# The second product's parts behind every second Strassen product instead of behind each

## The chip, the cores and the metric

One core of a Trainium2 chip runs the whole program. The metric is device time in microseconds (us) from launch to the last output, the median of several runs; three runs of the kernel before gave 844.39 to 845.39 us, median 845.2 us.

## What is computed

```python
ret = (q @ k.T / sqrt(64)) * Dmat          # decayed, causal, per head; B 4, H 8, S 576, D 64
x = (ret @ v), heads side by side          # 2304 tokens x 512
h = x @ w_in;  g = relu(h) ** 2            # 512 -> 2048
x = g @ w_out                              # 2048 -> 512
h = x @ w_in2; g = h * clip(h + 3, 0, 6) / 6
out = g @ w_out2
```

The weights come as 64-bit floats and are decoded on the chip. Every fp32 matrix product of the two layers is made from three matmuls with the operands split into a high and a low part (high x high, high x low, low x high: `PASSES`).

## The kernel before

After the retention the 2304 tokens are worked off in blocks of 768. The first block of layer 1 is done plainly, chunk by chunk. The other five (`BLOCKS`, L21: two of layer 1, three of layer 2) compute the hidden values by Strassen-Winograd's seven products instead of eight. The loop at L1022 runs over 40 pairs k of 128-wide hidden chunks, eight pairs to a block. Pairs 0 to 15 are of layer 1, 16 to 39 of layer 2.

One call of `pair` (L675) issues the seven products P1, P6, P2, P7, P5, P4, P3 in this order, each six matmuls of 384 columns (L690). They go in turn into two PSUM banks, `ta` and `tb` (P1, P2, P5, P3 in the one, P6, P7, P4 in the other), and each is read out right behind its matmuls, in the program's order: ACT copies P1 (`p1`, L725) and P2 (`c11`, L733); DVE adds P6, P7, P5, P4 and P3 to the running sums (L714). From the five sums come the four hidden tiles c11, u3, c21 and c12. `act` (L696) applies the nonlinearity: on ACT alone in layer 1 (L701, L702), on ACT and DVE in layer 2 (L706, L707). ACT then rounds the high part (L708), and DVE makes the low part (L710), one product later (`late`, `flush`): so the low part of c21 is issued on DVE right behind the addition for P3 (c12, L754, L755).

The second matrix product (g @ w_out) of a pair is held in `pending` as **parts** and issued during the next pair, in the gaps between its products, by `between(i)` behind product i. In layer 1 a pair has eight parts of six matmuls (three of 512 columns, three of 256; L478); in layer 2 twelve parts of three matmuls (512 columns; L650). The first half of the parts uses the tile g[1], made from u3 and c21; the second half uses g[0], from c11 and c12. The first matmul of a part reads a high part; the second one, in its operands, a low part. In the last pair of a block the sums of the second product end: these parts are issued in the next pair (k = 8, 16, 24, 32; for the plain block in pair 0), and each is followed by the copy of its PSUM bank to memory, on DVE (L485, L663) or ACT (L486, L490, L667).

`between(i)` also issues `side[i]`: pieces of the preparation of later blocks and of layer 2's weights (decoding, L171 to L190; splitting, L196 and L197; operand sums, L585, L602, L607), and DMAs on SP's queue. Every engine works off its instructions in the written order (`manual_schedule`, L777). Where a part stands therefore decides what PE does between two products, and, in pairs with PSUM copies, also what stands ahead of the next addition on DVE and ACT.

Of the kernel before, what the change touches and what calls it, by code (L numbers as in the profile page):

```python
# [74 lines left out]
def retention_moe_moe2(ctx, tc, qk, qk_last, kv, w_in, w_out, w_in2, w_out2, consts, out):  # L75
# [339 lines left out]
    def load_out(l, key, c):  # L415
        w = wout_place()
        nc.sync.dma_start(out=w.rearrange("p e n -> p (e n)").bitcast(F32), in_=kept["o", l, c])
        wouts[key] = w
# [48 lines left out]
    def y_first(t0, state):  # L467

        def work(w, gt, first, last):
            def step(m):  # L470
                if first and m == 0:
                    state["y"] = [bank(b, [128, 512], "yps") for b in range(KD)]
                    state["y"] += [bank(KD + b, [128, 2, 256], "ytail") for b in range(2)]
                y = state["y"]
                for k, (o, n) in enumerate(PARTS):
                    p = y[KD + m // 2][:, m % 2] if k else y[m]
                    for e, (wp, gpart) in enumerate(PASSES):
                        nc.tensor.matmul(  # L478
                            out=p, lhsT=w[:, wp, m * 128:m * 128 + 128], rhs=gt[:, gpart, o:o + n],
                            start=first and e == 0 and not (k and m % 2), stop=last and e == 2, skip_group_check=k == 1,  # L480
                        )
                if last:
                    dst = xall[:, m, t0:t0 + 512]
                    if m % 2:
                        nc.vector.tensor_copy(dst, y[m])  # L485
                        nc.scalar.activation(  # L486
                            out=xall[:, m - 1:m + 1, t0 + 512:t0 + BLOCK], in_=y[KD + m // 2], func=ACTF.Copy
                        )
                    else:
                        nc.scalar.activation(out=dst, in_=y[m], func=ACTF.Copy)  # L490

            return [lambda m=m: step(m) for m in range(KD)]

        return work
# [118 lines left out]
    def load_left(k):  # L613

        j, p = divmod(k, NPAIR)
        l = BLOCKS[j][0]
        lefts[j, p] = []
        for e in range(4):
            if l == 0 and e > 1:
                t = place(f"w{4 * (k % 2) + e}", [128, 2, 2, 256], F32R, "win")  # L620
                nc.sync.dma_start(
                    out=t[:, 1].rearrange("p a n -> p (a n)").bitcast(F32),
                    in_=kept["f", 0, p][:, 512 * (e - 2):512 * (e - 1)],
                )
                lefts[j, p].append(t.rearrange("p b a n -> p a b n"))
                continue
            only = slice(1, 2) if e == 1 else slice(0, 2)
            t = place(f"w{4 * (k % 2) + e}", [128, 1 if e == 1 else 2, 2, 256], F32R, "win")
            nc.sync.dma_start(
                out=t.bitcast(F32),  # L630
                in_=kept["s", l, p, e].rearrange("p (a b n) -> p a b n", a=2, b=2)[:, only],
            )
            lefts[j, p].append(t)

    def parts_of_left(k, e):

        hi, lo = (lefts[divmod(k, NPAIR)][e][:, :, wp] for wp in range(2))
        return split_parts(hi, lo, lo.bitcast(F32), nc.vector)

    def y_second(j, state):  # L640

        t0, n = BLOCKS[j][1], BLOCK

        def work(w, gt, first, last):
            def step(m):
                if first and m == 0:
                    state["y"] = [bank(b, [128, DM], "yps") for b in range(n // 128)]
                p = state["y"][m]
                for e, (wp, gpart) in enumerate(PASSES):
                    nc.tensor.matmul(  # L650
                        out=p, lhsT=gt[:, gpart, m * 128:m * 128 + 128], rhs=w[:, wp],
                        start=first and e == 0, stop=last and e == 2,
                    )
                if last:
                    if j == len(BLOCKS) - 1 and m < 4:
                        o = place(f"w{m}", [128, DM], F32, "o")
                    else:
                        o = stagep.tile([128, DM], F32, tag="stage", name="o")
                    final = j == len(BLOCKS) - 1
                    for f in range(2 if final and m == n // 128 - 1 else 1):  # L660
                        own = slice(256 * f, 256 * f + 256) if final and m == n // 128 - 1 else slice(0, DM)
                        if (m + f) % 2 == 0:
                            nc.vector.tensor_scalar(  # L663
                                out=o[:, own], in0=p[:, own], scalar1=1.0 / 6.0, scalar2=None, op0=ALU.mult
                            )
                        else:
                            nc.scalar.activation(out=o[:, own], in_=p[:, own], func=ACTF.Copy, scale=1.0 / 6.0)  # L667
                        queue = nc.scalar if final and (m + f) % 2 else nc.sync
                        queue.dma_start(out=out[t0 + m * 128:t0 + m * 128 + 128, own], in_=o[:, own])

            return [lambda m=m: step(m) for m in range(n // 128)]

        return work

    def pair(j, p, flip, between):  # L675

        wl = lefts.pop((j, p))
# [46 lines left out]
        product("P1", ta, True, False)  # L724
        nc.scalar.activation(out=p1, in_=ta, func=ACTF.Copy)  # L725
        between(0)
        tb = bank(b1, [128, HALF], "hps")
        product("P6", tb, True, True)
# [48 lines left out]
    with tc.manual_schedule():  # L777
# [52 lines left out]
        for k in range(2):  # L830
            kind, u, k = order.pop(0)
# [190 lines left out]
        for k in range(total):  # L1022
            j, p = divmod(k, NPAIR)
            l = BLOCKS[j][0]
            if p == 0:
                ywork = y_second(j, {}) if l else y_first(BLOCKS[j][1], {})
            side = [[] for _ in range(7)]


            if j + 1 < len(BLOCKS):  # L1030
                if p == 2:
                    sums, highs2, lows2 = operand_steps(j + 1)
                if 2 <= p < 5:
                    for i, f in zip((1, 4), sums[2 * (p - 2):][:2]):
                        side[i].append(f)
                if p == NPAIR - 1:
                    highs, lows = highs2, lows2
                    for i, at in enumerate((0, 1, 3, 4, 6)):
                        if at < 6:
                            side[at + 1].append(lows[i])  # L1040
                        side[at].append(highs[i])
                    side[6] += sums[6:]
            if p == 0:
                if j:
                    side[0].append(lows[4])
                else:
                    side[0] += sums[6:]
                for i, at in ((5, 1), (6, 3)):
                    side[at].append(highs[i])
                    side[at + 1].append(lows[i])  # L1050
            for i, e in ((4, 1), (6, 0)):
                side[i].append(lambda e=e: load_out(l, (j, 2 * p + e), 2 * p + e))
            if k >= 1 and k + 1 < total:
                side[0].append(lambda: load_left(k + 1))
            if k + 1 < total and BLOCKS[(k + 1) // NPAIR][0] == 0:
                for i, e in ((4, 2), (5, 3)):
                    for n in range(2):
                        side[i + n].append(lambda e=e, n=n: parts_of_left(k + 1, e)[n]())
            if p < NPAIR - 1:
                for i in range(4 if j and not p else 0, 7):  # L1060
                    if slots:
                        side[i] += [store_late] + slots.pop(0)
            elif late_stores:
                side[1].append(store_late)
            count = len(pending)

            def between(i):
                want = count - count * (i + 1) // 7
                while len(pending) > want:
                    pending.pop(0)()  # L1070
                for f in side[i]:
                    f()

            gt = pair(j, p, flip, between)
            flip = not flip
            assert not pending
            for e in (1, 0):
                pending += ywork(
                    wouts[j, 2 * p + e], gt[e], p == 0 and e == 1, p == NPAIR - 1 and e == 0
                )  # L1080
# [37 lines left out]
```

## Time and profile before

| what | value |
|---|---|
| median of 3 runs | 845.2 us (844.39 to 845.39) |
| the profiled execution | 845.26 us, its span 843.5 us |
| PE busy | 825.0 us, 98% of the span |
| DVE, ACT, POOL busy | 586.1 us, 466.6 us, 144.5 us |
| granted TensorE clock | 0.999 |
| pairs 0 to 39 | from 194.7 us on |

The profile has one execution. Times are counted from the first instruction. "Busy" of PE is the union of modelled matmul durations, which overlap: a 384-column matmul is shown with 338 ns, but the next one starts some 175 ns later. So the pace of PE is read from starts, not from durations. A release written behind an arrow ("<-DVE g L710") names the instruction whose end let the waiting one begin.

### The profile page before, as it was taken

The page shows a single profiled execution, that of the slowest core. Times are in us where ns is not written, and L with a number is a line of the kernel's source. Part 1 is how long each engine was busy: PE and PEld are TensorE (multiplying, and loading weights), DVE is VectorE, ACT ScalarE, POOL GpSimd, SP SyncE. Part 2 cuts the span into 40 slices and gives each one's busy share as a digit, 9 for nine tenths or more (in the row PEclk, how much of TensorE's full clock was granted, in tenths as well). Part 3 has the DMA queues.
Part 4 walks back from the last instruction along what each step waited for, and adds up shares of the span by engine and source line. Part 5 has one row for each costly group of instructions (what it writes and reads, how often), then busy time and mean ns, then how long its engine had stood idle before and what let it go on. Part 6 is the DMA issues. An engine that isn't in the chain of part 4 may idle for free.

```text
span 843.5 us, 14173 instructions
## 1 busy us (share of the span) xinstructions
PE 825.0 (98%) x5220; PEld 741.9 (88%) x5220; DVE 586.1 (69%) x1018; ACT 466.6 (55%) x913; POOL 144.5 (17%) x122
## 2 busy tenths in 40 slices
PE   8989999997999999999999999999999999999998
PEld 7878888886999899999999888898898888889886
DVE  5779999999787876887875895546644546534434
ACT  1248777768865876867775653335433345433332
POOL 2353333331332320132230130000000000000000
PEclk9999999999999999999999999999999999999999
DMA  9996788876787894689786688553854552854522
GB/s 364 343 300 221 239 289 282 294 249 242 258 326 275 304 330 177 232 280 362 276 293 266 225 287 312 202 185 137 316 221 163 188 199 87 329 209 161 201 99 75
DMA packets 77963, 206.58 MB, mean 245 GB/s; under 512 B 8005, under 2 KB 24773, under 8 KB 77895
## 3 DMA queue, kind: packets, MB, share of 16 engines
q1 hardware_dynamic: 77314, 204.90, 68.9%
q8 instruction: 41, 0.67, 0.3%
q10 hardware_dynamic: 580, 0.79, 0.3%
q14 instruction: 28, 0.22, 0.1%
HBM read 159.00 MB, written 46.66 MB: 244 GB/s over the span
## 4 chain that ended last, share of the span: by engine, by line
PE 80%; DVE 7%; DMA 6%; ACT 4%; issue 1%; SPq 1%; POOL 0%; DVEq 0%; ACTq 0%; POOLq 0%
PE hps L690 33%; PE yps L650 22%; PE yps L478 13%; PE ytail L478 7%; PE hps L431 5%; DMA kvt<-in_kv_dram 3%; DMA qkt<-in_qk_dram 3%; DVE a L184 1%; DVE g L454 1%; DMA stage<-in_w_out_dram 1%; DVE w L190 1%; DVE a L178 1%; ACT u L706 0%; ACT r L172 0%; DVE u L714 0%
## 5 line engine op out<-in xcount | busy, mean ns | idle before, releaser
L650 PE MATMUL yps<-wo,g 128*128 128x512 f32 x864 | 226.8, 394 | 1.5 <-DVE g L710 1.3
L690 PE MATMUL hps<-xlast,win 128*128 128x384 f32 x960 | 194.9, 338 | 1.7 <-DVE u L714 1.6
L650 PEld LDWEIGHTS yps<-wo,g 128*128 128x128 f32 x864 | 159.4, 188 | 26.0 <-DVE g L710 2.0
L690 PEld LDWEIGHTS hps<-xlast,win 128*128 128x128 f32 x960 | 167.7, 188 | 10.5 <-DVE u L714 2.1
L714 DVE TENSOR_TENSOR u<-hps,u 128x384 f32<-128x384 f32 x120 | 66.8, 557 | 157.1 <-PE hps L690 150.5
L478 PE MATMUL yps<-g,wo 128*128 128x512 f32 x576 | 166.1, 396 | 0.4 <-POOL wo L197 0.4
L690 PE MATMUL hps<-xop,win 128*128 128x384 f32 x720 | 146.4, 338 | 3.7 <-ACT r L447 3.4
L690 PEld LDWEIGHTS hps<-xop,win 128*128 128x128 f32 x720 | 125.7, 188 | 10.7 <-ACT r L447 3.6
L708 ACT ACTIVATE g<-c 128x384 fp32r<-128x384 f32 x120 | 63.1, 525 | 88.1 <-DVE c L707 86.6
L478 PEld LDWEIGHTS yps<-g,wo 128*128 128x128 f32 x576 | 101.8, 188 | 10.2 <-POOL wo L197 0.8
L478 PEld LDWEIGHTS ytail<-g,wo 128*128 128x128 f32 x576 | 94.0, 188 | 17.3
L478 PE MATMUL ytail<-g,wo 128*128 128x256 f32 x576 | 98.5, 279 | 0.0
L710 DVE TENSOR_TENSOR g<-c,g 128x384 fp32r<-128x384 f32 x120 | 67.9, 566 | 11.3 <-ACT g L708 11.1
L431 PE MATMUL hps<-xring,win 128*128 128x512 f32 (+1 forms) x384 | 69.7, 338 | 0.3 <-ACT r L447 0.2
L733 ACT ACTIVATE c<-hps 128x384 f32<-128x384 f32 x40 | 19.7, 492 | 90.9 <-PE hps L690 90.9
L431 PEld LDWEIGHTS hps<-xring,win 128*128 128x128 f32 x384 | 60.1, 190 | 8.7 <-ACT r L447 0.7
L706 ACT ACTIVATE u<-c,three 128x384 f32<-128x384 f32 x72 | 44.4, 617 | 31.7 <-DVE c L714 30.5
L714 DVE TENSOR_TENSOR c<-hps,u 128x384 f32<-128x384 f32 x80 | 44.3, 554 | 21.8 <-PE hps L690 21.7
L184 DVE SCALAR_TENSOR_TENSOR a<-stage,a 128x512 int32<-128x512 int32 x64 | 51.2, 800 | 0.9
L707 DVE SCALAR_TENSOR_TENSOR c<-u,c 128x384 f32<-128x384 f32 x72 | 41.3, 574 | 13.5 <-ACT u L706 13.4
L171 ACT ACTIVATE a<-stage 128x512 f32<-128x512 f32 x64 | 42.4, 663 | 6.4 <-DMA stage<-in_w_in_dram 6.4
L172 ACT ACTIVATE r<-stage 128x512 int32<-128x512 uint32 x64 | 42.2, 660 | 0.0
(97 smaller groups left out, 905.5 us busy)
## 6 DMA issues: line engine op xcount, KB each, us to landing
win<-kept SPq DMA_DIRECT2D x88, 512.0 KB
wo<-kept SPq DMA_DIRECT2D x80, 512.0 KB
kept<-ready SPq DMA_DIRECT2D x40, 512.0 KB
win<-kept SPq DMA_DIRECT2D x72, 256.0 KB
stage<-in_w_out_dram SPq DMA_DIRECT2D x32, 512.0 KB
kept<-wo SPq DMA_DIRECT2D x16, 512.0 KB
stage<-in_w_in_dram SPq DMA_DIRECT2D x16, 512.0 KB
qkt<-in_qk_dram SPq DMA_DIRECT2D x13, 512.0 KB
```

The costliest lines, as they stand in the source:

```text
L171: nc.scalar.activation(out=a, in_=high.bitcast(F32), func=ACTF.Abs)
L172: nc.scalar.activation(out=r, in_=low.bitcast(U32), func=ACTF.Copy, scale=2.0 ** -29)
L184: nc.vector.scalar_tensor_tensor(out=a.bitcast(I32), in0=high, scalar=-0x40000000, in1=a.bitcast(I32), op0=ALU.bitwise_and, op1=ALU.bitwis ...
L431: nc.tensor.matmul(out=h, lhsT=w[:, kk // 2, wp, kk % 2 * 128:][:, :128], rhs=xs[kk][xp][:, o:o + n], start=m == 0, stop=m == 3 * KD - 1,)
L478: nc.tensor.matmul(out=p, lhsT=w[:, wp, m * 128:m * 128 + 128], rhs=gt[:, gpart, o:o + n], start=first and e == 0 and not (k and m % 2), s ...
L650: nc.tensor.matmul(out=p, lhsT=gt[:, gpart, m * 128:m * 128 + 128], rhs=w[:, wp], start=first and e == 0, stop=last and e == 2,)
L690: nc.tensor.matmul(out=to, lhsT=wl[k][:, half if k != 1 else 0, wp, o], rhs=x[:, xp, f], start=first and m == 0, stop=last and m == 5, ski ...
L706: nc.scalar.activation(out=v, in_=c, func=ACTF.Relu, bias=three)
L707: nc.vector.scalar_tensor_tensor(out=c, in0=v, scalar=6.0, in1=c, op0=ALU.min, op1=ALU.mult)
L708: nc.scalar.activation(out=hi, in_=c, func=ACTF.Copy)
L710: lambda: nc.vector.tensor_tensor(out=lo, in0=c, in1=hi.bitcast(F32), op=ALU.subtract)
L714: nc.vector.tensor_tensor(out=out_, in0=to, in1=x, op=ALU.add)
```

## The change

`want` is the number of parts that may be left when `between(i)` returns. Before, it fell behind every product, in near-equal steps over the seven. Now it falls only behind those products whose count over all pairs, 7k + i, is odd: i = 1, 3, 5 in even pairs and i = 0, 2, 4, 6 in odd ones. In the other places all that is left stays.

```diff
             def between(i):
-                want = count - count * (i + 1) // 7
+                groups = [n for n in range(7) if (7 * k + n) % 2]
+                if i not in groups:
+                    want = count
+                else:
+                    want = count - count * (groups.index(i) + 1) // len(groups)
                 while len(pending) > want:
                     pending.pop(0)()
                 for f in side[i]:
```

Parts behind P1, P6, P2, P7, P5, P4, P3, before and now (the two kinds of pairs have the same order before):

| pair | before | now |
|---|---|---|
| 8 parts, even | 1 1 1 1 1 1 2 | 0 2 0 3 0 3 0 |
| 8 parts, odd | 1 1 1 1 1 1 2 | 2 0 2 0 2 0 2 |
| 12 parts, even | 1 2 2 1 2 2 2 | 0 4 0 4 0 4 0 |
| 12 parts, odd | 1 2 2 1 2 2 2 | 3 0 3 0 3 0 3 |

The `side` pieces stay behind their products. On PE, from P4 of pair 0 to the first part of pair 1, before (`xlast` holds the operands of P7, P5, P4, P3, `xop` those of P1, P6, P2; L478 are the parts):

```order
L690 MATMUL hps<-xlast,win 128x384 x6
L478 MATMUL yps<-g,wo 128x512 x3
L478 MATMUL ytail<-g,wo 128x256 x3
L690 MATMUL hps<-xlast,win 128x384 x6
L478 MATMUL yps<-g,wo 128x512 x3
L478 MATMUL ytail<-g,wo 128x256 x3
L478 MATMUL yps<-g,wo 128x512 x3
L478 MATMUL ytail<-g,wo 128x256 x3
L690 MATMUL hps<-xop,win 128x384 x6
L478 MATMUL yps<-g,wo 128x512 x3
L478 MATMUL ytail<-g,wo 128x256 x3
```

and now, from P5 and P4 (one row of twelve) of pair 0 on:

```order
L690 MATMUL hps<-xlast,win 128x384 x12
L478 MATMUL yps<-g,wo 128x512 x3
L478 MATMUL ytail<-g,wo 128x256 x3
L478 MATMUL yps<-g,wo 128x512 x3
L478 MATMUL ytail<-g,wo 128x256 x3
L478 MATMUL yps<-g,wo 128x512 x3
L478 MATMUL ytail<-g,wo 128x256 x3
L690 MATMUL hps<-xlast,win 128x384 x6
L690 MATMUL hps<-xop,win 128x384 x6
L478 MATMUL yps<-g,wo 128x512 x3
L478 MATMUL ytail<-g,wo 128x256 x3
```

The two parts that stood between P3 of the even pair and P1 of the odd pair have moved ahead of P3; between P3 and the first part of the odd pair P1 alone is left.

On DVE nothing moves but the PSUM copies of the block changes. In pair 8, from the addition for P4 (L714) on; L485 is the copy of a finished PSUM bank:

```order
 L714 TENSOR_TENSOR c<-hps,u 128x384
 L710 TENSOR_TENSOR g<-u,g 128x384
-L485 COPY xall<-yps 128x512
-L197 TENSOR_TENSOR win<-win 128x512
-L184 SCALAR_TENSOR_TENSOR a<-stage,a 128x512
-L714 TENSOR_TENSOR c<-hps,u 128x384
-L710 TENSOR_TENSOR g<-c,g 128x384
-L485 COPY xall<-yps 128x512
+L485 COPY xall<-yps 128x512 x2
+L197 TENSOR_TENSOR win<-win 128x512
+L184 SCALAR_TENSOR_TENSOR a<-stage,a 128x512
+L714 TENSOR_TENSOR c<-hps,u 128x384
+L710 TENSOR_TENSOR g<-c,g 128x384
```

The second copy, which stood behind the addition for P3 (the second L714) and the low part of c21 (the second L710), stands ahead of both now. On ACT the copies L490 and L486 move ahead of c12's nonlinearity in the same way. The order on SP and POOL stays.

## Rows read from the trace of the kernel before

**Rows 1.** The page: busy time of each engine, and the chain that ended last

```profile
PE 825.0 (98%) x5220; PEld 741.9 (88%) x5220; DVE 586.1 (69%) x1018; ACT 466.6 (55%) x913; POOL 144.5 (17%) x122
...
PE 80%; DVE 7%; DMA 6%; ACT 4%; issue 1%; SPq 1%; POOL 0%; DVEq 0%; ACTq 0%; POOLq 0%
```

**Rows 2.** Timeline of PE, pairs 12 and 13: start us, us, engine, line, operation, tiles, xcount

```profile
399.16 1.23 PE L690 MATMUL hps<-xlast,win 128*128 128x384 f32 x6
400.23 0.87 PE L478 MATMUL yps<-g,wo 128*128 128x512 f32 x3
...
401.28 1.23 PE L690 MATMUL hps<-xlast,win 128*128 128x384 f32 x6
402.35 0.87 PE L478 MATMUL yps<-g,wo 128*128 128x512 f32 x3
...
404.44 1.21 PE L690 MATMUL hps<-xop,win 128*128 128x384 f32 x6
405.49 0.86 PE L478 MATMUL yps<-g,wo 128*128 128x512 f32 x3
```

**Rows 3.** Timeline of PE in layer 2, pair 27

```profile
633.61 1.21 PE L690 MATMUL hps<-xlast,win 128*128 128x384 f32 x6
634.65 0.86 PE L650 MATMUL yps<-wo,g 128*128 128x512 f32 x3
635.35 1.22 PE L690 MATMUL hps<-xlast,win 128*128 128x384 f32 x6
636.41 1.55 PE L650 MATMUL yps<-wo,g 128*128 128x512 f32 x6
637.80 1.21 PE L690 MATMUL hps<-xlast,win 128*128 128x384 f32 x6
```

**Rows 4.** Timeline from P3 of pair 28 to P1 of pair 29

```profile
655.92 1.21 PE L690 MATMUL hps<-xlast,win 128*128 128x384 f32 x6
...
657.17 0.56 DVE L714 TENSOR_TENSOR c<-hps,u 128x384 f32<-128x384 f32 x1 [0.57 <-PE hps L690]
...
657.64 0.55 DVE L710 TENSOR_TENSOR g<-c,g 128x384 fp32r<-128x384 f32 x1
...
658.36 1.20 PE L690 MATMUL hps<-xop,win 128*128 128x384 f32 x6
```

**Rows 5.** Timeline from P3 of pair 18 to the first part of pair 19

```profile
497.94 0.68 PE L690 MATMUL hps<-xlast,win 128*128 128x384 f32 x3
...
500.89 0.45 PE L650 MATMUL yps<-wo,g 128*128 128x512 f32 x1
501.17 1.10 DVE L710 TENSOR_TENSOR g<-c,g 128x384 fp32r<-128x384 f32 x1
...
502.32 0.73 PE L650 MATMUL yps<-wo,g 128*128 128x512 f32 x2 [0.97 <-DVE g L710]
```

**Rows 6.** Timeline of DVE, pair 8 (block change), from P5's addition to P3's

```profile
334.69 0.56 DVE L714 TENSOR_TENSOR u<-hps,u 128x384 f32<-128x384 f32 x1 [1.56 <-PE hps L690]
...
337.37 0.55 DVE L714 TENSOR_TENSOR c<-hps,u 128x384 f32<-128x384 f32 x1
...
338.30 0.68 DVE L485 COPY xall<-yps 128x512 f32<-128x512 f32 x1
...
340.10 0.55 DVE L714 TENSOR_TENSOR c<-hps,u 128x384 f32<-128x384 f32 x1
```

**Rows 7.** Timeline of DVE, pair 10, the additions for P5, P4 and P3

```profile
366.60 0.56 DVE L714 TENSOR_TENSOR u<-hps,u 128x384 f32<-128x384 f32 x1 [0.36 <-PE hps L690]
...
370.32 0.54 DVE L714 TENSOR_TENSOR c<-hps,u 128x384 f32<-128x384 f32 x1
...
372.46 0.55 DVE L714 TENSOR_TENSOR c<-hps,u 128x384 f32<-128x384 f32 x1
```

**Rows 8.** Timeline of PE, pair 0: P7 behind its wait

```profile
203.27 1.32 PE L690 MATMUL hps<-xlast,win 128*128 128x384 f32 x6 [1.56 <-DVE u L714]
```

**Rows 9.** Timeline of the weight loads, pair 5: P2 behind ACT's copy of P1

```profile
281.15 1.00 PEld L690 LDWEIGHTS hps<-xop,win 128*128 128x128 f32 x6 [0.34 <-ACT u L725]
```

## The prediction

> **What bounds the kernel now.** The page comes first: PE is busy 98% of the span, DVE 69%, and 80% of the chain that ended last is PE's [rows 1]. The change moves nothing but PE's instructions, apart from some PSUM copies. So only two things can change the time: the pace of PE inside a group of matmuls, and the places where PE waits for DVE or ACT. I read the first from PE's timeline, start to start, in a stretch without waits; the second from the timeline of all engines around the places where the distance between a product and its reader's consumer becomes shorter.
>
> **Pace.** In layer 1 [rows 2] a product that follows a single part takes 1.07 us to the next group's start (399.16 to 400.23), a part 1.05 us (to 401.28). Two parts in a row take 2.09 us (402.35 to 404.44), and the product behind them only 1.05 us (to 405.49). So longer groups run a little faster. A pair of eight parts costs 6 x 1.07 + 1.05 + 6 x 1.05 + 2.09 = 15.86 us before. Regrouped, with all products at 1.05 us and parts at 2.09 / 2 = 1.045 us, it costs 7 x 1.05 + 8 x 1.045 = 15.71 us: 0.15 us less. In layer 2 [rows 3] a product takes 1.04 us behind two parts (633.61 to 634.65) and 1.06 us behind one (635.35 to 636.41); one part takes 0.70 us, two 1.39 us. Before: 2 x 1.06 + 5 x 1.04 + 2 x 0.70 + 5 x 1.39 = 15.67 us; regrouped 7 x 1.04 + 12 x 0.695 = 15.62 us: 0.05 us less. Seventeen pairs issue eight parts (0 to 16), 23 issue twelve: 17 x 0.15 + 23 x 0.05 = **3.7 us gained**. One thing here no row shows: a product directly behind a product, 3.5 in a pair on average. I take it at the value behind a long group, since the six matmuls ahead of it are such a group too. The other end is that it costs as much as behind a single part, 0.02 us more: 40 x 3.5 x 0.02 = 2.8 us, and the gain is 0.9 us.
>
> The Trainium skill ("TensorE: Matmul & The Clock Gate", Back-to-back issue gap) has the gap between warm matmuls as the columns over 2.4 GHz plus about 2.5 ns, whatever came before. By that rule (an estimate from the page: 0.975 us for a product) regrouping gains nothing, and the sum below would be 3.7 us higher. The trace has 1.04 to 1.07 us, and a dependence on the group ahead, so I go by the rows.
>
> **The new wait: the first part of an odd pair.** The first part of a pair needs, at its second matmul, the low part of c21. DVE makes it behind the addition for P3, which needs P3's end. Before, two parts and P1 stood between P3 and that part. Now, wherever an even pair goes over into an odd one (20 times), only P1 does. How long DVE needs is in [rows 4], where nothing else is in its way: P3 ends at 655.92 + 1.21 = 657.13, the addition starts at 657.17, and the low part is done at 657.64 + 0.55 = 658.19, **1.06 us behind P3's end**. How long PE can go on is calibrated by a wait that exists already [rows 5]: P3 of pair 18 ends at 498.62, the first part starts at 500.89, 2.27 us later. The low part, late there, is done at 502.27, 3.65 us behind P3's end. The part's second matmul, due 0.23 us behind the first, starts at 502.32, 1.20 us late, and the matmul behind it loses 0.1 us more (two take 0.73 us there, three take 0.86 us in [rows 3], so two should take 0.63 us): 1.30 us in all. So the stall is the low part's lag less the part's start less 0.08 us: 3.65 - 2.27 - 0.08. With P1 alone in between, the part starts 0.88 us behind P3's modelled end (a start 0.17 us behind P3's last, 1.04 us of P1, less the 0.34 us that a matmul is shown to last). PE stalls for lag - 0.96 us, at the least 1.06 - 0.96 = 0.10 us. Eighteen boundaries (the other two, into pairs 5 and 19, wait already and are taken as unchanged, because their chains come from ACT and DVE work that the change doesn't move) cost 18 x 0.10 = **1.8 us**. Bounds: 0 if P1 turns out 0.1 us longer, 0.15 us each.
>
> **Where DVE is behind when P3 ends.** The lag is longer where DVE still has work. Two effects go against each other in even pairs: P5 is one part later than before (1.05 us in layer 1), and all that hangs on it moves with it; P3 is two parts later (2.1 us). So a lag that is driven from P5 shrinks by 1.05 us.
>
> - *Block changes* (pairs 0, 8, 16, 24, 32). In pair 8 the addition for P4 starts 337.37 - 334.69 = 2.68 us behind that for P5 [rows 6]; now P4 ends only 1.05 us behind P5, so this work sets it. From there to the addition for P3 took 2.73 us, with one copy in it (338.30); from that copy to the addition 1.80 us. Now both copies stand ahead, and the second waits for the third part, which ends some 4.2 us behind P5's end (1.05 for P4, 3.15 for three parts). It starts at about 4.25, and the addition 1.80 us later, at 6.05. P3 ends at 1.05 + 3.15 + 1.05 = 5.25 us. So the addition is 0.8 us late, the lag 1.06 + 0.8 us, the stall 0.8 us above the least. I take **0.75 us for each of five, 3.75 us**. Between 0 (the copy meets a gap) and 1.5 us (in pair 16 DVE has the step L707 of layer 2 as well).
> - *Pairs 10 and 12*, with slow decoding: from P5's addition to P4's 3.72 us, to P3's 2.14 us more [rows 7], 5.86 us; P3 ends at 5.25 us, so the lag is 0.6 us above the least: **2 x 0.6 = 1.2 us**. Between 0 (the slow instructions there were slow beside POOL) and 1.6 us.
> - Other even pairs have less than 5.2 us of DVE work from P5 on: nothing above the least.
>
> **Pair 0.** P7 starts there after a wait of 1.56 us for the addition of P6 [rows 8], which DVE reaches late because of its own queue, so at the same time as now. Before, one part stood between P2 and P7; now none: PE has a part less (1.05 us) to cover it with: **1.05 us**. Between 0 and 1.05 us, since what is covered later is not lost only if a later wait exists to take it.
>
> **ACT's copy of P1 in odd pairs.** P2 may only start when ACT has copied P1 out. In pair 5 that is late already and costs 0.34 us [rows 9]. P1 follows P3 more closely now, and c12's nonlinearity, three ACT instructions, stands ahead of the copy. P1 to P2 keeps its two parts and one product. I take 0.1 us in five pairs of layer 1, **0.5 us**; bounds 0 and 2 us.
>
> **Nothing** is taken for the other readers: between a product and the next user of its bank there are still a product and a group of two parts or more (three or more in layer 2), about 3.1 us, as before. SP's and POOL's orders are unchanged.
>
> **The sum:** -3.7 + 1.8 + 3.75 + 1.2 + 1.05 + 0.5 = +4.6 us against the profiled execution's 845.26 us, 849.9 us. The median of the runs is 0.06 us below that execution, which changes nothing: **849.9 us**, 0.55% slower. A measurement of this kernel can tell about 0.2% (1.7 us) from no change.
>
> **The rivals.**
>
> 1. *Faster.* The regrouping pays and the low part of c21 is in time. The point that decides is 0.96 us of lag: the quiet 1.06 us misses it by only 0.1 us, and the third part ahead of P3 gives DVE 1.05 us more to catch up on the chain from P5. If the block changes and pairs 10 and 12 catch up altogether, what is left is -3.7 + 0.5 to 1.8: 842 to 843.4 us. Against it: the copies stand ahead of the addition and can't start before the parts end. Chance 0.12.
> 2. *No change.* Least stalls and pair 0 come true, half of the lags don't: -3.7 + 1.8 + 1.05 + 0.5 + half of 4.95, about +2, less if the gain is full everywhere: 844.5 to 846.9 us. Chance 0.18.
> 3. *Slower still by SP's queue.* The weights of the pair after next are loaded into buffers that P3 frees. In even pairs P3 is 2.1 us later (1.39 us in layer 2), and so is all that is queued behind on SP: stores that free the split buffers, loads of raw weights. Where ACT waits for those, its chain moves by up to 2.1 us and with it c21. For two or three pairs of layer 1: 853 to 856 us. For it speaks that 6% of the chain is DMA [rows 1]; against, that loads are asked for a pair ahead. Chance 0.15.
> 4. *No gain from grouping*, the case of the skill's rule: what makes the product faster behind two parts is not the grouping, so each takes its present time: 849.9 + 3.7 = 853.6 us, or 850.8 to 853.6 with part of it. Against it: [rows 2, 3] agree. Chance 0.10.
>
> **How the numbers follow.** The forecast has 0.45, with its own range 847 to 853 us from the bounds of its terms. Slower by over 0.2%: 0.45 + 0.15 + 0.10 = 0.70; within: 0.18; faster: 0.12. The range leaves out the greater part of the first rival and the far end of the third: 844.3 to 855.0 us.
>
> **What would show it.** Right: in the timeline, groups of twelve matmuls of 384 columns at 2.09 us and single parts gone; in quiet pairs of layer 2 a first part of odd pairs whose second matmul waits about 0.1 us for DVE L710; waits of about 0.9 us there in pairs 1, 9, 17, 25, 33, and of 0.7 us in 11 and 13; P7 of pair 0 behind a wait of about 2.6 us. In the view of waits, "PE or PEld yps <- DVE g L710" becomes the largest wait of PE, 8 us or more. Wrong: no waits at those places (then it is faster), or waits at P2, or for DMA, in many pairs.

## The result, and the profile after

The changed kernel takes 852.0 us (median of four runs, 851.3 to 854.4) against 845.3 us of the kernel before beside it (four runs, 844.39 to 846.48): ratio 1.009 [1.007, 1.0109], 0.9% slower. The forecast was 849.9 us, slower. The profiled execution took 851.3 us, its span is 849.5 us.

The page after, busy time of each engine and the chain that ended last:

```profile
PE 827.0 (97%) x5220; PEld 740.3 (87%) x5220; DVE 587.1 (69%) x1018; ACT 467.2 (55%) x913; POOL 140.6 (17%) x122
...
PE 77%; DVE 8%; ACT 6%; DMA 5%; issue 3%; POOL 1%; SPq 0%; ACTq 0%; DVEq 0%; POOLq 0%
```

The counts are those of [rows 1]: the work is the same. PE's share of the chain fell from 80% to 77%, DVE's and ACT's rose: PE waits for them in more places. Which places, the view of waits tells from 210 us on (us in total, times, longest). The kernel before, on PE and its weight loads:

```profile
PE yps L650 <- DVE g L710: 1.3, 2, 1.0
...
PEld yps L650 <- DVE g L710: 2.0, 2, 1.3
...
PEld hps L690 <- ACT u L725: 0.5, 2, 0.3
...
PEld yps L478 <- DVE g L710: 0.4, 1, 0.4
```

and after:

```profile
PE yps L650 <- DVE g L710: 3.7, 4, 1.6
PE yps L478 <- DVE g L710: 2.4, 4, 0.9
...
PEld yps L650 <- DVE g L710: 7.0, 13, 2.0
PEld yps L478 <- DVE g L710: 4.9, 8, 1.3
PEld hps L690 <- ACT u L725: 2.6, 6, 0.5
```

The weight load of a part's second matmul, which needs the low part of c21 (L710), waits 21 times (11.9 us) instead of 3 (2.4 us). P2's load behind ACT's copy of P1 (L725) waits 6 times instead of 2. It is the largest wait of the loads, as the prediction had it. The loads run ahead of their matmuls, so PE itself loses less.

**The account.** From pair 0's first matmul to the last matmul of the kernel the profiled execution before took 644.36 us, the one after 652.42 us: +8.05 us. (Ahead of pair 0 the executions differ by 2.0 us the other way, where nothing was changed, so the two spans differ by only 6.0 us.) I split this by the starts of PE's matmuls: what a distance has above the usual one (174 ns at 384 columns, 231 to 233 at 512, 117 at 256), if that is over 30 ns, is time lost, the rest pace. A pair is called quiet where DVE starts P3's addition within 0.04 us of P3's end.

| term, us | before | after | difference | in the sum |
|---|---|---|---|---|
| pace, layer 1 (17 pairs) | 269.39 | 266.62 | -2.77 | -2.55 |
| pace, layer 2 (23 pairs) | 368.71 | 368.41 | -0.30 | -1.15 |
| first part, 11 quiet pairs (3, 11, 13, 21, 23, 27, 29, 31, 35, 37, 39) | 0 | 1.16 | +1.16 | +2.3, of it 1.2 in 11 and 13 |
| first part, pairs 1, 9, 17, 25, 33 | 1.20 | 5.39 | +4.19 | +4.25 |
| first part, pairs 7 and 15 | 0 | 2.14 | +2.14 | +0.2 |
| pairs 5 and 19 but for P2 | 2.06 | 2.21 | +0.15 | 0 |
| P2 of odd pairs behind ACT | 0.64 | 2.31 | +1.67 | +0.5 |
| P6 of even pairs 10, 12, 14, 18 | 0 | 0.76 | +0.76 | 0 |
| pair 0 | 2.38 | 3.42 | +1.04 | +1.05 |
| together | | | +8.04 | +4.6 |

Of pair 0's 3.42 us after, 1.55 are a fall of the granted clock that the other execution didn't have (last section).

**Pace.** PE's timeline in pair 13, the columns as in [rows 2]:

```profile
408.42 2.27 PE L690 MATMUL hps<-xop,win 128*128 128x384 f32 x12
410.54 0.86 PE L478 MATMUL yps<-g,wo 128*128 128x512 f32 x3
...
412.62 2.25 PE L690 MATMUL hps<-xlast,win 128*128 128x384 f32 x12
414.71 0.86 PE L478 MATMUL yps<-g,wo 128*128 128x512 f32 x3
```

Two products in a row take 2.09 us (412.62 to 414.71), as forecast; two parts behind them 2.08 us (410.54 to 412.62). In layer 1 a quiet even pair went from 15.85 to 15.67 us.

**A quiet boundary**, pair 28 into 29, all engines, to be set beside [rows 4]:

```profile
657.05 2.27 PE L690 MATMUL hps<-xlast,win 128*128 128x384 f32 x12
...
659.15 2.92 PE L650 MATMUL yps<-wo,g 128*128 128x512 f32 x12
...
661.92 1.23 PE L690 MATMUL hps<-xlast,win 128*128 128x384 f32 x6
...
662.98 1.20 PE L690 MATMUL hps<-xop,win 128*128 128x384 f32 x6
663.18 0.56 DVE L714 TENSOR_TENSOR c<-hps,u 128x384 f32<-128x384 f32 x1 [0.83 <-PE hps L690]
...
663.65 0.55 DVE L710 TENSOR_TENSOR g<-c,g 128x384 fp32r<-128x384 f32 x1
...
664.02 2.34 PE L650 MATMUL yps<-wo,g 128*128 128x512 f32 x9
664.26 1.69 PEld L650 LDWEIGHTS yps<-wo,g 128*128 128x128 f32 x8 [0.22 <-DVE g L710]
```

P3 ends at 661.92 + 1.23 = 663.15, and DVE, which was waiting for it, has the low part at 664.20. The first part began at 664.02; the weights of its second matmul can be loaded only at 664.26. The two matmuls are 337 ns apart instead of 231: 0.106 us lost, where the sum had 0.10. The products ahead, in layer 2, took 2.10 us for two, no less than two apart did (1.04 and 1.06 in [rows 3]).

**A block change**, pair 8 into 9:

```profile
339.24 1.28 DVE L485 COPY xall<-yps 128x512 f32<-128x512 f32 x2
...
339.61 1.21 PE L690 MATMUL hps<-xlast,win 128*128 128x384 f32 x6
...
340.43 0.68 DVE L197 TENSOR_TENSOR win<-win 128x512 fp32r<-128x512 f32 x1
...
341.03 0.68 DVE L184 SCALAR_TENSOR_TENSOR a<-stage,a 128x512 int32<-128x512 int32 x1
...
341.63 0.55 DVE L714 TENSOR_TENSOR c<-hps,u 128x384 f32<-128x384 f32 x1
...
342.10 0.55 DVE L710 TENSOR_TENSOR g<-c,g 128x384 fp32r<-128x384 f32 x1
...
342.71 0.73 PE L478 MATMUL yps<-g,wo 128*128 128x512 f32 x2 [0.61 <-DVE g L710]
```

Both copies and two instructions more stand between P4's addition and P3's. P3 ends at 340.82, its addition starts 0.81 us later (forecast: 0.8), the low part is there at 342.65, and PE loses 0.88 us.

The calibration of the prediction, stall = lag of the low part behind P3's end less 0.96 us, held to 0.02 us at all twenty boundaries; four of them:

| into pair | P3 ends | low part done | lag | less 0.96 | lost on PE |
|---|---|---|---|---|---|
| 29 | 663.15 | 664.20 | 1.05 | 0.09 | 0.11 |
| 9 | 340.82 | 342.65 | 1.83 | 0.87 | 0.88 |
| 15 | 436.90 | 439.05 | 2.15 | 1.19 | 1.19 |
| 17 | 469.44 | 472.29 | 2.85 | 1.89 | 1.90 |

### The profile page after: what moved, and what is told of

Read it like the earlier page. It is cut to its first block, busy times and chain, and to the rows that moved or that the text cites. A ratio compares the mean times of both kernels' runs of the same rounds, so it can differ in the third digit from the quotient of the medians.

```text
span 849.5 us, 14173 instructions
## 1 busy us (share of the span) xinstructions
PE 827.0 (97%) x5220; PEld 740.3 (87%) x5220; DVE 587.1 (69%) x1018; ACT 467.2 (55%) x913; POOL 140.6 (17%) x122
## 4 chain that ended last, share of the span: by engine, by line
PE 77%; DVE 8%; ACT 6%; DMA 5%; issue 3%; POOL 1%; SPq 0%; ACTq 0%; DVEq 0%; POOLq 0%
PE hps L690 29%; PE yps L650 21%; PE yps L478 12%; PE ytail L478 6%; PE hps L431 5%; DMA kvt<-in_kv_dram 2%; DMA kept<-ready 2%; ACT u L706 1%; PE vps L343 1%; PE aps L327 1%; DMA qkt<-in_qk_dram 1%; ACT a L171 1%; ACT r L172 1%; DVE xlast L607 1%; DVE a L184 1%
## 5 line engine op out<-in xcount | busy, mean ns | idle before, releaser
L650 PE MATMUL yps<-wo,g 128*128 128x512 f32 x864 | 214.3, 394 | 4.2 <-DVE g L710 3.7
L690 PE MATMUL hps<-xlast,win 128*128 128x384 f32 x960 | 184.0, 336 | 1.5 <-DVE u L714 1.5
L714 DVE TENSOR_TENSOR u<-hps,u 128x384 f32<-128x384 f32 x120 | 66.6, 555 | 149.5 <-PE hps L690 147.5
L478 PE MATMUL yps<-g,wo 128*128 128x512 f32 x576 | 167.0, 397 | 3.0 <-DVE g L710 2.4
L690 PE MATMUL hps<-xop,win 128*128 128x384 f32 x720 | 142.5, 340 | 4.2 <-ACT r L447 3.5
L478 PEld LDWEIGHTS yps<-g,wo 128*128 128x128 f32 x576 | 98.4, 189 | 14.4 <-DVE g L710 4.9
L478 PEld LDWEIGHTS ytail<-g,wo 128*128 128x128 f32 x576 | 94.2, 188 | 16.6
L478 PE MATMUL ytail<-g,wo 128*128 128x256 f32 x576 | 98.8, 280 | 0.0
L710 DVE TENSOR_TENSOR g<-c,g 128x384 fp32r<-128x384 f32 x120 | 68.4, 570 | 13.2 <-ACT g L708 11.8
L714 DVE TENSOR_TENSOR c<-hps,u 128x384 f32<-128x384 f32 x80 | 44.2, 553 | 32.8 <-PE hps L690 32.8
L184 DVE SCALAR_TENSOR_TENSOR a<-stage,a 128x512 int32<-128x512 int32 x64 | 51.9, 811 | 0.9
L707 DVE SCALAR_TENSOR_TENSOR c<-u,c 128x384 f32<-128x384 f32 x72 | 40.7, 566 | 13.8 <-ACT u L706 12.9
```

What stands on the lines that cost most here:

```text
L184: nc.vector.scalar_tensor_tensor(out=a.bitcast(I32), in0=high, scalar=-0x40000000, in1=a.bitcast(I32), op0=ALU.bitwise_and, op1=ALU.bitwis ...
L478: nc.tensor.matmul(out=p, lhsT=w[:, wp, m * 128:m * 128 + 128], rhs=gt[:, gpart, o:o + n], start=first and e == 0 and not (k and m % 2), s ...
L650: nc.tensor.matmul(out=p, lhsT=gt[:, gpart, m * 128:m * 128 + 128], rhs=w[:, wp], start=first and e == 0, stop=last and e == 2,)
L690: nc.tensor.matmul(out=to, lhsT=wl[k][:, half if k != 1 else 0, wp, o], rhs=x[:, xp, f], start=first and m == 0, stop=last and m == 5, ski ...
L707: nc.vector.scalar_tensor_tensor(out=c, in0=v, scalar=6.0, in1=c, op0=ALU.min, op1=ALU.mult)
L710: lambda: nc.vector.tensor_tensor(out=lo, in0=c, in1=hi.bitcast(F32), op=ALU.subtract)
```

## The experiments

Every experiment edits `between` of the changed kernel, but for two that say so. Theory A in the expectations is that of the prediction: the regrouping gives pace, and the loss is new waits, first of all that of an odd pair's first part for the low part of c21, since P1 alone is left between P3 and it; what a rival makes of a run stands beside it. Each ratio is against runs of the kernel before on the same chip, medians of 844.44 us (experiments 1 to 4), 844.65 us (5 to 8) and 844.5 us (9 and 10). "Lost" is time lost by the account above, in the Strassen pairs of the profiled execution (before: 6.3 us; the change: 17.4 us).

**1. The same groups in every pair.** A part group stands behind P3 always, so no product pair bridges two pairs.

```diff
-                groups = [n for n in range(7) if (7 * k + n) % 2]
+                groups = [1, 3, 5, 6]
```

> Groups behind P6, P7, P4 and P3 of every pair: P3 always has parts behind it, so between the end of P3 and the first part of the next pair stand a group of parts, P1 and P6. Theory A (the loss is the wait of the first part in odd pairs for the low part of c21, queued on DVE behind P3's addition): that wait is gone in all 39 boundaries, also those in pairs 17 and 19 that the kernel before has; the faster pace stays (layer 1 products in twos at 2.09 us). Faster than before: 840 to 843.5 us. Theory B (P3 being later in its pair holds up SP's queue and with it the split buffers and ACT): P3 is as late in every pair here (all parts but the last group stand ahead of it), so ACT's waits for buffers stay and the time is 847 us or more. Theory C (longer groups are no faster by themselves): 845 us or more.

Measured: 845.19 us, ratio 1.0005 [0.9992, 1.0018]. The first-part waits are gone, "yps <- DVE g L710" is not in the view of waits. But three others grew, so that 11.5 us are lost still, 4.9 of them in pair 0. The waits of the weight loads for products in the view of waits, and P7 of pair 0 in PE's timeline:

```profile
PEld hps L690 <- DVE u L714: 3.7, 4, 1.5
PEld hps L690 <- ACT u L725: 1.9, 4, 0.8
```

```profile
202.26 2.29 PE L690 MATMUL hps<-xlast,win 128*128 128x384 f32 x6 [2.61 <-DVE u L714]
```

In an odd pair P7 now has four parts between it and the even pair's P3, where the kernel before has five, and DVE's own queue is no earlier. (P2's waits for ACT don't follow from the parts ahead of it, four in both; they stay open.) Pair 0 has the change's order up to P4; its 4.9 us are mostly P7's wait, 2.77 us by the starts, and a fall of the clock behind it, of which the last section tells. The run shows where the first-part waits come from (take the bridge away, and they go), and that another grouping puts others in their place. The forecast of a gain missed. The time is one that theory C allows, but C is out by the pace: layer 1's is 3.1 us better than before.

**2. The low part ahead of the addition** (in `pair`, L754, L755).

```diff
-        add(c12, ta, u2)
         flush()
+        add(c12, ta, u2)
```

> The change, with DVE's low part of c21 issued ahead of the addition for P3 instead of behind it; nothing else. Theory A: the low part no longer waits for P3's end. In quiet pairs the first part's wait of 0.106 us goes to 0 (12 boundaries, 1.3 us), and where DVE is behind it shrinks by the 0.48 us that the addition takes (8 boundaries, 3 to 4 us): 847 to 848.5 us. Theory B (SP and the buffers): no change, 851 to 853 us, and the waits in pairs 7, 15, 17, 19 stay as long as they are.

Measured: 854.18 us, ratio 1.0106 [1.0081, 1.0131], lost 20.3 us. The quiet waits of 0.106 us went to nothing (two quiet pairs of layer 2 take 31.35 instead of 31.45 us), and pair 9's fell from 0.88 to about 0.4 us, so the low part's lag is what PE waited for there. But DVE works in order and now waits for ACT's high part ahead of the addition that frees P3's bank. DVE's timeline, pair 28 into 29, and the view of waits:

```profile
667.83 0.56 DVE L710 TENSOR_TENSOR g<-c,g 128x384 fp32r<-128x384 f32 x1 [0.59 <-ACT g L708]
668.30 0.55 DVE L714 TENSOR_TENSOR c<-hps,u 128x384 f32<-128x384 f32 x1
```

```profile
PEld hps L690 <- ACT u L725: 7.0, 9, 1.3
...
PE hps L690 <- DVE c L714: 2.4, 4, 1.1
```

c12, which ACT works on ahead of its copy of P1, comes later, and P2 waits for the copy. The wait moved from the part to the product: outside pair 0 the profiled execution loses 15.4 us, the change's 14.0. By their times (the ratios' intervals overlap) the two can't be told apart. A's forecast of a gain missed.

**3. The other phase**, parts behind even counts, so that the bridge lies between odd and even pairs.

```diff
-                groups = [n for n in range(7) if (7 * k + n) % 2]
+                groups = [n for n in range(7) if (7 * k + n) % 2 == 0]
```

> The change with the count the other way round: groups behind i = 0, 2, 4, 6 in even pairs and 1, 3, 5 in odd ones. P3 and P1 are then neighbours where an odd pair goes over into an even one; the block changes and their PSUM copies (pairs 0, 8, 16, 24, 32) keep parts behind P3. Theory A: the least wait of 0.106 us stays at 19 boundaries (2 us), but in odd pairs DVE is less behind at P3, and no copy stands ahead of the addition, so the waits of 0.8 to 1.9 us in pairs 1, 9, 17, 25, 33 go, and so do those of the kernel before in 17 and 19: 842 to 845.5 us. Theory B (SP's queue behind a late P3): the delay comes in odd pairs instead, 848 us or more.

Measured: 855.54 us, ratio 1.0124 [1.01, 1.0149], lost 20.1 us. The quiet waits moved as A says: 0.1 us in the first part of pairs 2, 4, 6, 8, 22, 26, 28 and others, none in the quiet odd pairs of layer 2. But the time was missed by 10 us, because products that now come earlier found their operands late:

```profile
PEld hps L690 <- ACT u L725: 3.3, 6, 1.2
PEld hps L690 <- DVE xlast L607: 3.1, 3, 1.2
PEld hps L690 <- DVE u L714: 2.9, 3, 1.5
```

The second row is new: DVE's operand sums of the next block (L607), needed in pairs 16, 24 and 32. The time lies in theory B's range, and over half of the loss is in odd pairs, as B has it. But what PE waited for there is ACT and DVE, and ACT's waits for stores that free a split buffer (three, in pairs 2, 4 and 6) last 11.0 us, where the kernel before has 9.1; that the loss comes from SP's queue is not shown.

**4. The block changes in the old order** (`p` is the pair's number within its block).

```diff
-                if i not in groups:
+                if p == 0:
+                    want = count - count * (i + 1) // 7
+                elif i not in groups:
```

> The change, but pairs 0, 8, 16, 24 and 32 (the first of a block, with the PSUM copies) keep the order of before. Theory A: the waits of pairs 1, 9, 17, 25, 33 (0.88, 1.36, 1.90, 1.21, 1.22 us) fall to those of before (0, 0.23, 0.63, 0.36, 0.21), and pair 0 waits 1 us less; the rest stays: 852.0 - 5.1 - 1 is 846 us. Theory B: those waits come from a late P3 on SP, of which there are 15 left, so at most half of it goes: 849 us or more.

Measured: 846.83 us, ratio 1.0026 [1.0012, 1.004], where A had put it. Lost 10.6 us. Pairs 1, 9, 17, 25 and 33 lose 0, 0.27, 0.99, 0.41 and 0.08 us instead of 0.88, 1.36, 1.90, 1.21 and 1.22; the 0.106 us of the quiet pairs and 1.20 us in pair 15 stay. Of the 6.8 us that it loses less than the change, 4.8 are in these five pairs and 1.0 in pair 0, which has its old order too: five pairs of forty carry most of the loss.

**5 and 6. One layer alone.** Experiment 5 keeps the old order where `count == 12`, experiment 6 where `count == 8`:

```diff
-                if i not in groups:
+                if count == 12:
+                    want = count - count * (i + 1) // 7
+                elif i not in groups:
```

> The change where a pair issues eight parts (pairs 0 to 16), the order of before where it issues twelve (17 to 39). By the trace of the change, layer 1's stretch gains 3.4 us of pace and waits 1 us longer in pair 0 and 3.6 us longer in 1 to 16, and pair 17's first wait hangs on pair 16; layer 2's part of the loss, with waits of 0.1 us at ten boundaries, 1.2 us in 25 and 33, 0.4 us in 18, 0.5 us more in 19, is some 4 us. Theory A (each wait comes from the distances in its own pair): 847 to 849 us. Theory B (a delay in layer 1 is handed on through the DMA queue into layer 2): 850 us or more.

> The change where a pair issues twelve parts (17 to 39), the order of before in pairs 0 to 16. Theory A: pace in layer 2 gains only 0.2 us, the waits there cost 3 to 4 us more: 847.5 to 849.5 us. Theory B (the pace that the rows of before promised for layer 2, 1.15 us, is there): 846.5 us or less.

Measured: layer 1 alone 849.86 us, ratio 1.0069 [1.0049, 1.0088]; layer 2 alone 848.45 us, ratio 1.0043 [1.0028, 1.0058]. Above 844.65 us these are 5.2 and 3.8 us, 9.0 together, where the whole change's interval reaches from 5.9 to 9.2 us (0.7% to 1.09%): both layers lose, and layer 2 has next to no pace to set against its waits. Layer 1 came out a little above what A had and just below B. In its profiled execution the pairs from 18 on, all in the old order, lose 2.6 us, where the kernel before loses 1.9: at most 0.7 us were handed on.

**7. Four groups, and P3 and P1 never together, in layer 1.** Even pairs take parts behind P6, P7, P4 and P3, odd ones behind P1, P2, P5 and P3. Pair 0 and layer 2 keep the old order.

```diff
-                groups = [n for n in range(7) if (7 * k + n) % 2]
-                if i not in groups:
+                groups = [0, 2, 4, 6] if k % 2 else [1, 3, 5, 6]
+                if k == 0 or count == 12:
+                    want = count - count * (i + 1) // 7
+                elif i not in groups:
```

> In pairs 1 to 16 four groups of two parts each: behind P6, P7, P4, P3 in even pairs, behind P1, P2, P5, P3 in odd ones. P3 always has parts behind it, so a group and P1 stand between P3 of an even pair and the first part of the odd one, as before; ACT's late copy of P1 in odd pairs keeps a group and a product before P2, and P7 keeps two groups behind P6. Pair 0 and layer 2 as before. Theory A: the pace of layer 1 (3.2 us) comes without new waits: 841 to 843 us, faster than before. Theory B (longer groups bring their own waits wherever they are, by DVE's work coming in bursts): 844 us or more.

Measured: 843.02 us, ratio 0.9977 [0.9967, 0.9987]: faster than the kernel before. PE's timeline in pair 11:

```profile
373.30 2.25 PE L690 MATMUL hps<-xop,win 128*128 128x384 f32 x12
375.39 0.86 PE L478 MATMUL yps<-g,wo 128*128 128x512 f32 x3
...
377.48 2.25 PE L690 MATMUL hps<-xlast,win 128*128 128x384 f32 x12
```

A quiet layer-1 pair takes 15.65 us, pace is up by 3.0 us in the layer (269.39 to 266.36), and 7.8 us are lost, 1.5 more than before (0.5 of it in pair 0, whose order is the old one); "yps L478 <- DVE g L710" is gone from the waits. The pace is real, and can be had without the bridge.

**8. The same in both layers**, pair 0 as before:

```diff
-                if k == 0 or count == 12:
+                if k == 0:
```

> The same four groups in layer 2 as well (three parts each), pair 0 as before. Theory A: pace in layer 2 is worth nothing (products in twos cost 2.106 us there, 1.049 us each before), waits none: within 0.7 us of e7, 841 to 843.5 us. Theory B (bursts): 844 us or more.

Measured: 842.87 us, ratio 0.9978 [0.9967, 0.999], as experiment 7. Pace in layer 2 is 369.29 us, 0.6 us slower than before. Grouping is worth nothing in layer 2.

**9. POOL's first split on DVE** (`split_left`, the engine that makes the low part of a new weight tile, for the tiles with k = 0).

```diff
-nc.gpsimd)
+nc.gpsimd if k else nc.vector)
```

> The change, with the first of the four low-part splits of a layer 2 weight pair on DVE instead of POOL (eight instructions of some 0.7 us moved). In the change's trace the low part of c21 in pair 14 takes 1.63 us beside such a split on POOL, 0.55 us otherwise, and pair 15 waits 1.19 us. Theory A (the wait of pair 15 is this collision): pair 15's first part waits 0.1 to 0.5 us; elsewhere DVE has 0.7 us more per pair in pairs 3 to 17, so the time may stay near 852 us. Theory B (the wait of pair 15 is P3's lateness handed on): it still waits 1 us or more.

This is about pair 15, which the prediction had as quiet. Timeline of the change, POOL and DVE, pair 14 into 15:

```profile
437.36 1.28 POOL L197 TENSOR_TENSOR ready<-wd,ready 128x512 fp32r<-128x512 f32 x1 [4.01 <-ACT ready L196]
437.42 1.63 DVE L710 TENSOR_TENSOR g<-c,g 128x384 fp32r<-128x384 f32 x1
```

The low part of c21 takes 1.63 us instead of 0.55 beside POOL's instruction. Before the change the same POOL instruction (436.06 to 437.70) fell on another DVE instruction, and the low part took 0.54 us:

```profile
435.40 0.54 DVE L710 TENSOR_TENSOR g<-c,g 128x384 fp32r<-128x384 f32 x1
...
436.47 1.78 DVE L190 CUSTOM_DVE_ANT_0 wd<-a,r 128x1024 uint16<-128x1024 uint16 x1
```

Measured: 857.39 us, ratio 1.0155 [1.0139, 1.0172]. With POOL out of the way the duration is back, but the moved split stands ahead of P3's addition on DVE and waits for ACT:

```profile
444.02 0.69 DVE L197 TENSOR_TENSOR ready<-wd,ready 128x512 fp32r<-128x512 f32 x1 [1.08 <-ACT ready L196]
444.63 0.55 DVE L714 TENSOR_TENSOR c<-hps,u 128x384 f32<-128x384 f32 x1
445.10 0.55 DVE L710 TENSOR_TENSOR g<-c,g 128x384 fp32r<-128x384 f32 x1
```

PE loses 1.09 us there still, 1.55 us each in pairs 11 and 13, and 4.5 us in pair 9 (of it 1.6 us by a fall of the clock behind 2.64 us of idle PE). The wait is what theory B forecast, but its cause is the moved split, which the change doesn't have. So the run shows where the low part's 1.1 us came from, but by its time it says nothing of what the collision cost.

**10. Pair 0 in the old order.**

```diff
-                if i not in groups:
+                if k == 0:
+                    want = count - count * (i + 1) // 7
+                elif i not in groups:
```

> The change, with pair 0 in the order of before. Theory A (a part less stands between P2 and P7 of pair 0, whose start is set by DVE): 1 us less, and where the longer idle time costs granted clock in a run, up to 2.5 us less: 849.5 to 851 us. Theory B (the later parts of pair 0 take the wait back): no change, 852 us.

Measured: 851.07 us, ratio 1.0078 [1.0064, 1.0091]. That is 1 us below the change's 852.03, at the upper end of what A has, but the two ratios' intervals overlap, so it is weak evidence of a term of 1 us.

## Why the prediction was right, and where it was not

The sign, the mechanism and the size of its largest terms were right; it was 2.1 us low against the median. Against the account it was 3.4 us low (4.6 for 8.05), of which 1.55 are the clock. In its own order:

- **Pace**: 3.07 us gained, 3.7 forecast. Layer 1 gave 2.77 (2.55 forecast). Layer 2 gave 0.30, not 1.15: the mis-sized term is a product behind a long group at 1.04 us, read in [rows 3] behind six matmuls and carried over to groups of nine and twelve. There it measured 1.066 us. The step that no row showed, a product directly behind a product, was right: 1.040 us in both layers. The fourth rival, with the rule of the Trainium skill ("TensorE: Matmul & The Clock Gate", Back-to-back issue gap) beside it, falls in layer 1 and comes near the truth in layer 2. The section gives that gap for an isolated matmul, and says that in a stream of weight loads and matmuls both set the spacing. The rows lie above the isolated gap: 1.040 to 1.066 us a product, by what stood ahead, where its figure makes 0.975 (an estimate).
- **The new wait, least case**: 0.106 us against 0.10, in 11 of 18 pairs. The other seven lose more, for the reasons below.
- **Block changes**: +4.19 us against 5 x 0.85 = 4.25. Right in sum, less so one by one. Pairs 1 and 9 lose 0.88 each, as forecast. Pair 17 loses 1.90, above even the bound of 1.5 plus 0.1: L707 of layer 2 (469.00, the step that the bound names), two copies and L184 put P3's addition 1.83 us behind P3's end. And 17, 25 and 33 had lost 0.63, 0.36 and 0.21 us before, which the prediction overlooked when it wrote that only pairs 5 and 19 wait already. The two errors cancel. Experiment 4 shows the term by taking it away.
- **Pairs 10 and 12**: wrong, 0.1 us each instead of 0.7. The additions for P5, P4 and P3 in pair 10, to be set against [rows 7]:

```profile
368.46 0.56 DVE L714 TENSOR_TENSOR u<-hps,u 128x384 f32<-128x384 f32 x1 [1.77 <-PE hps L690]
...
371.21 0.55 DVE L714 TENSOR_TENSOR c<-hps,u 128x384 f32<-128x384 f32 x1
...
373.69 0.56 DVE L714 TENSOR_TENSOR c<-hps,u 128x384 f32<-128x384 f32 x1 [0.26 <-PE hps L690]
```

  From the first to the second now 2.75 us, not 3.72: the decoding (L175, L178) takes 0.41 and 0.43 us, where it took 0.96 and 0.84. POOL's L510 and L511 ran beside them before (368.18 to 370.11); now L511 ended at 370.09, ahead of them. The prediction named this as the lower bound and took the upper half: it treated a chance coincidence with POOL as a property of the instructions.
- **Pairs 7 and 15**: missed, 2.1 us. In 15 POOL's instruction now falls on the low part of c21. Beside pairs 10 and 12: PE shifted by a microsecond, a slow spell went in one place and another came elsewhere. In pair 7 ACT comes late with c21. Its splitting of a weight tile (L196) starts 11.7 us into pair 6, where it had started 10.1 us in, and c21's nonlinearity stands behind. ACT's row before, after, and in experiment 10, which has the change's order there:

```profile
303.36 0.63 ACT L196 ACTIVATE ready<-sums 128x512 fp32r<-128x512 f32 x1 [3.01 <-DMA kept<-ready]
```

```profile
303.94 0.63 ACT L196 ACTIVATE ready<-sums 128x512 fp32r<-128x512 f32 x1 [4.65 <-DVE g L710]
```

```profile
301.73 0.63 ACT L196 ACTIVATE ready<-sums 128x512 fp32r<-128x512 f32 x1 [3.23 <-DMA kept<-ready]
```

  The split waits for the store (L412) that frees its buffer. By the trace's semaphore times the store had landed at 303.28 us before and at 303.86 after, 0.08 us ahead of the split each time; L710, which the second row names, ended beside it by chance. The landing varies from execution to execution, and the loss with it: in five executions with the change's order in pairs 6 and 7 (the change, experiments 4, 5, 9 and 10) the split starts 11.7, 10.9, 11.3, 10.3 and 10.3 us into pair 6, and pair 7's first part loses 0.95, 0.21, 0.60, 0.11 and 0.11 us. Pair 5 hangs on such a store in pair 4 in the same way, before the change too; the prediction took its chain for ACT's and DVE's work.
- **ACT's copy of P1**: under-sized. 0.5 us was forecast with a bound of 2; P2 of odd pairs lost 1.67 us more, in 3, 5, 7, 9, 25 and 33. Experiments 1 to 3 show the same wait at other sizes: the copy stands behind c12's nonlinearity, and that behind P3.
- **"Nothing" for the other readers**: wrong by 0.8 us, in P6 of pairs 10, 12, 14 and 18. In layer 1 "as before" doesn't hold for P6: between an odd pair's P3 and the next P6, in the same bank, stood three parts and P1, and stand two parts and P1 now. In pair 12 P6's load waits for ACT's split of a weight tile; 10 and 14 lose 0.07 us each, which stays open. In pair 18, of layer 2, it waits for that P3's addition, which DVE reaches late: L707 (486.29) had waited 1.34 us for ACT.
- **Pair 0**: right in sum (+1.04, forecast 1.05), but the profile of after doesn't show the step. Nearly half of the loss is the clock there (last section), and P7 waited 1.49 us rather than 2.6. That the sum agrees is luck. In experiment 1, which orders pair 0 alike up to P4, PE came at full clock, and P7 did wait 2.61 us. Over the profiled executions pair 0 loses 2.4 to 2.8 us in the old order (before, 4, 6, 7, 8, 10), 3.4 us in the change's (the change, 5, 9) and 4.95 us in 1 and 2.

Of the rivals, the first and second fall by the ratio (the second's own sum, +2.1, makes 847.4 us, above the range it was given). The third had ACT held up by late stores and loads behind P3, for 853 to 856 us. ACT's wait for a store is there, in pair 6, and is worth 0.95 us in this execution. But that store was issued 0.03 us behind the split on DVE that fills its buffer (295.50 and 295.53 us; 295.41 and 295.44 before), so it was not held behind P3; why it took 8.3 us to land, and 7.8 before, is open. PE itself waited for a DMA once, 0.5 us. The rest of the time between forecast and result comes from DVE, ACT and the clock.

## What to carry to other kernels

A regrouping on one engine changes the slack of every reader and writer at once. Price each hand-over by the lag of the thing waited for less the work that now stands in between; a wait that exists already in the trace calibrated that to 0.02 us here. Before a group that spans two stages is taken, look at what the first instruction of the next stage reads: here four groups of two with a break at that place kept all of layer 1's pace, added 1.1 us of lost time outside pair 0 instead of 10.1, and were 0.2% faster than the kernel before.

## What the runs showed of the hardware

**A 128x384 subtraction on DVE took 1.63 us beside POOL's L197, and 0.55 us without**: it ends 0.41 us behind the modelled end of POOL's (437.36 + 1.28 = 438.64, 439.05). The Trainium skill ("SBUF — State Buffer", SBUF: two separate sides) says that DVE and GpSimd share a port pair, that of a DVE instruction with two inputs in SBUF and a GpSimd instruction that reads SBUF the one that starts first holds it for its whole length, and that the other is blocked. The trace agrees, as closely as spans on POOL are known: POOL's began 0.06 us earlier.

**The granted clock fell behind idle stretches of PE, but not behind each.** Busy time by stretch in the kernel before, after, and in experiment 1 (length, PE, PEld, DVE, ACT, POOL, granted clock, DMA share, GB/s):

```profile
192.00:197.00 5.00, 2.30 (x13) 2.17 (x14) 4.80 (x9) 4.87 (x12) 0.86 (x1) 1.00 0.05 14
```

```profile
192.00:197.00 5.00, 4.30 (x15) 4.11 (x16) 4.97 (x10) 4.94 (x13) 1.29 (x1) 0.66 0.05 16
```

```profile
202.00:207.00 5.00, 4.74 (x19) 4.35 (x20) 3.66 (x8) 3.70 (x8) 0.00 (x0) 0.66 0.99 320
```

Ahead of pair 0 PE was idle for 3.43 us before and for 3.46 us after. The first time the clock stayed at 2.4 GHz; the second time matmuls of 384 columns, from 193.5 us on, came 320 ns apart (1.2 GHz) and pair 0 lost 1.55 us by it. In experiment 1 it stayed up there and fell behind P7's 2.61 us instead. All twelve profiled executions have this idle stretch (3.43 to 3.46 us): in eight the clock fell within 1.6 us of pair 0's first matmul, among them four with the old order of pair 0 (6, 7, 8, 10); in four it didn't (before, 1, 2, 4). So the fall is not the change's doing, and one execution's price of such a wait is uncertain by 1.6 us.

**A matmul's pace depends on what stood ahead of the group, by 2 to 3%**, and not only by its length: a product took 1.044 us behind six matmuls of 512 columns, 1.062 behind three, 1.066 behind nine or twelve, and 1.040 behind another product. I have no explanation of the order of these.
